# Chunked attention and a feed-forward block: the third tile's first matmul in seven block products throughout

## The chip, the cores and the metric

The kernel runs on one core of a Trainium2 chip. A core has a matrix engine (TensorE, PE in the profile; its weight loads are listed as PEld), a vector engine (VectorE, DVE), an engine for activation functions (ScalarE, ACT), a general one (GpSimd, POOL) and SyncE (SP), which here issues nearly all transfers. Every engine has its own queue and works it off in order; semaphores tie the queues together. SBUF is the core's working memory, PSUM the small memory of eight banks into which TensorE writes.

The metric is the device time of one execution in microseconds. A comparison of two kernels takes runs of both on the same chip.

## The reference

Inputs are q, k, v of shape (8, 8, 576, 64), that is batch, heads, positions, head size, and two matrices w_in (512 x 2048) and w_out (2048 x 512). Attention is inside chunks of 64 positions, and a feed-forward block with the exact GELU follows:

```python
scores = scale * np.matmul(q_c, k_c.transpose(0, 1, 2, 4, 3))   # per chunk of 64 positions
attn = softmax(scores)                                          # over the last axis
x = matmul(attn, v_c)  ->  rows of (batch, position), columns of (head, 64): 4608 x 512
h = x @ w_in                                                    # "mm1", 4608 x 2048
g = 0.5 * h * (1.0 + erf(h * inv_sqrt2))
out = g @ w_out                                                 # "mm2", 4608 x 512, float32
```

## The kernel before

The 4608 rows are worked off as nine tiles of 512 rows: tiles 0 to 7 take the first 512 positions of each batch entry, tile 8 the last 64 positions of all eight. The "third tile" of the change is tile 2. The main loop runs over the tiles `t`; one turn (`phase`) is mm1 of tile `t` with GELU, then mm2 of tile `t`, and between the matmuls of the turn stands the attention of the following tile(s), so that x of tile `t + 1` is ready when the turn ends. The program is written in the order in which each engine is to run it; the framework adds the semaphores.

**Seven products.** From tile 1 on, mm1 is computed by the Winograd form of Strassen's scheme: x, w_in and h are cut into 2 x 2 blocks, and seven block products with sums of blocks stand for eight. `x_sums` makes the sums of x (T1 to T4) on DVE, `w_in_sums` those of w_in once. The columns of h are cut into four groups of two 128-column blocks in each half, called a, b, c and d. A product such as `6a` is four matmuls of 256 columns (L680). For each group: products 1 and 2 build bank X; `c1` copies X (after product 1) to bank Y on ACT, onto which 6, 5 and 3 are added; `c2` (ACT) and `c3` (DVE) take copies of Y on the way; products 7 and 4 build bank Z; `a2` and `a1` (DVE) add Z to those copies; `g..` are the GELUs on ACT that write h. So product 6 needs `c1`, product 5 may only be added once `c2` has read Y, product 3 once `c3` has, and product 4 once `a1` has read Z.

**The order.** Each tile has a string of such words, which `mm1_groups` (L649) follows: `LATE` for tile 1, `THIRD` for tile 2, `FOUR` for tiles 3 to 7, `LAST` for tile 8. In `FOUR` all four groups are in seven products. In the `THIRD` of before, groups a, b and c are, and group d's four 128-column blocks are computed plainly, at the word `p`: four matmuls of 512 columns into one bank (L702) and one GELU (L706). `FOURS` tells for which tiles bank Z lies in the PSUM pool of the transposes and which scratch tiles the groups use.

**What else stands in tile 2's turn.** `extra` ties other work to words of the string; the dictionary `e1` at L1109 to L1123 makes it for tile 2:

- `w_sums((4,))` at the first `1a`: the last of four sums of w_out blocks, one DVE instruction (L743). It is read by mm2 of tile 3, which is in seven products too (mm2 of tile 2 is plain).
- `in_order(3, g)` at the words `i0` to `i3`: k of tile 3 has been transposed by a DMA (`flip`, L197, `k_u<-k_nat`) with its keys in another order than that of the scores; four DVE copies (L205) write them in order to `k_t`. Tile 3 alone needs this here.
- behind the fourth copy (`behind_k`): a copy of one element on POOL (L1116), which holds POOL back until then, the POOL casts of tile 4's q and k to bf16 (L164), the two transposing DMAs of tile 4 on SP (L197), loads of v of tile 4 and q of tile 5, and the casts of v of tile 4 (L217).

In tile 2's mm2 (L867, sixteen slots of four matmuls of 512 columns), the scores of tile 3 (`quad_S`, L246) come ahead of slot 2, their sums on DVE (L270 on) follow, the products with v (L315) come ahead of slot 7, then x of tile 3 and `x_sums(3)`, and the scores of tile 4 in two halves ahead of slots 12 and 13. In tile 3's mm2 the scores of tile 5 follow in the same way.

Of the kernel before, what the change touches and what calls it, by code (L numbers as in the profile page):

```python
# [11 lines left out]
def kernel(  # L12
# [9 lines left out]
    nc = tc.nc  # L22
# [5 lines left out]
    B, H, S, D = q.shape  # L28
    CH = 64
    NC = S // CH  # L30
    J = 4
    PC = CH // J
    G = H // 2
# [56 lines left out]
    tiles = [dict() for _ in range(NT)]  # L90
# [108 lines left out]
    def in_order(t, g):  # L199

        st = tiles[t]
        if "k_u" not in st:
            st["k_u"], st["kt"] = st["kt"], flips.tile([P, G * J, P], bf16, tag="kt", name="k_t")
        raw = st["k_u"]
        DV(st["kt"][:, g * J:(g + 1) * J].rearrange("p n (e j) -> p (n e) j", j=J),  # L205
           raw[:, g * J:(g + 1) * J].rearrange("p j e -> p e j"))

    def cast_v_rows(t, copy, behind=None):
# [256 lines left out]
    def att_sum_pe(t, g):  # L465

        pT = tiles[t]["pT", g]
        sT = ps_at.tile([P, 2, MT // P // 2, 2], f32, tag="at", name="sT")
        for r in range(2):
            for m in range(2):  # L470
                nc.tensor.matmul(sT[:, r, m], pT[:, r, 2 * m:2 * m + 2].rearrange("p n e -> p (n e)"), ones_r[:],
                                 start=True, stop=True)
        rr = work.tile([P, 2, MT // P // 2, 2], f32, tag="rr", name="rr", bufs=2)

        def inverse():
            nc.vector.reciprocal(rr[:], sT[:])

        def spread():
            rc_ps = ps_mm.tile([P, CT // 2, 2, CH], f32, tag="mm", name="rc_ps")
            for m in range(2):  # L480
                for c in range(2):
                    for r in range(2):
                        nc.tensor.matmul(rc_ps[CH * r:CH * (r + 1), 2 * m:2 * m + 2, c],
                                         rr[:, r, m, c:c + 1].to_broadcast([P, D]), ident_f[:],
                                         start=True, stop=True, tile_position=(0, CH * r))
            nc.scalar.copy(rc_of(t, g), rc_ps[:].rearrange("p n c e -> p (n c e)"))
        return inverse, spread
# [27 lines left out]
    DV, AC, PO = nc.vector.tensor_copy, nc.scalar.copy, nc.gpsimd.tensor_copy  # L515
# [40 lines left out]
    FIRST7, FIRST71 = 3, 1  # L556
# [57 lines left out]
    def x_sums(t, which=(1, 3, 2, 4)):  # L614
# [7 lines left out]
        for i in which:  # L622
# [7 lines left out]
    LATE = """begin start sums 1a c1a p 1b 7a c1b 6a 2a c2a 2b g11a 5a 6b g11b c2b c3a a1a 1c c1c 7b 5b g22a 6c 4a  # L630
              c2c 3a c3b a2a 3b 5c 7c g12a a1b c3c 2c 4b 3c a1c g21a g12b 4c g22b a2b a2c g11c g21c g21b g12c
              g22c end"""

    THIRD = """begin 1a c1a p 1b c1b 2a 7a 6a c2a 6b 2b 5a g11a c2b g11b 1c c1c c3a a1a p 5b 4a g22a 6c a2a 2c c3b
               g11c 7b a1b i0 3a c2c 3b 7c g21a 5c i1 c3c a1c g12b g12a g22b p 4b g22c p 4c a2b a2c i2 i3 3c g21b
               g12c g21c"""

    LAST = """begin 1a c1a p 6a 1b c2a c1b 7a 2a 5a 6b g11a c2b c3a 1c 2b c1c g11b 5b a1a g22a 4a 6c 7b c2c 3a a2a
              c3b g21a g12a p a1b 4b 5c g22b 2c a2b 7c g21b g11c 3b c3c 3c a1c 4c g12b a2c h1 g22c g12c g21c p p
              h2 h3"""  # L640
# [1 line left out]
    FOUR = """begin 1a 1b c1a 1c 6a 7a c1b c2a 6b 5a 2a c1c 6c c2b 5b 7b c3a g11a a1a c3b c2c 3a a1b 1d 4a g22a 4b  # L642
               g12a c1d 2b a2a g22b 6d 5c g21a a2b 2d 7c h1 g11b c3c c2d 2c g11d 5d a1c 7d c3d 3c g21b 4c g11c 3b a1d
               g22c 4d g12c g12b 3d a2c a2d g21c g22d g12d g21d h2 h3"""

    FOURS = range(FIRST7, B)
    PROGRAMS = {1: LATE, 2: THIRD, B: LAST, **{t: FOUR for t in FOURS}}

    def mm1_groups(t, extra, between={}):  # L649

# [6 lines left out]
        banks, sums = {}, {}  # L657
        four = t in FOURS
        tags = {"a": ("y_1", "y_2"), "b": ("y_5", "rc" if four else "y_2"), "d": ("y_1", "rc")}
# [28 lines left out]

        for word in PROGRAMS.get(t, PROGRAM).split():
            for u in extra.pop(word, ()):  # L690
# [42 lines left out]
    def w_sums(which):  # L733

        b11, b12 = w_out_sb[:, :FH, :NH], w_out_sb[:, :FH, NH:]
        b21, b22 = w_out_sb[:, FH:, :NH], w_out_sb[:, FH:, NH:]
        for i in (1, 3):
            if i in which:
                pair = wsum.tile([P, 2, FH, NH], bf16, tag="wsum", name="w_t")
                w_t[i], w_t[i + 1] = pair[:, 0], pair[:, 1]  # L740
        of = {1: (b12, b11), 3: (b22, b12), 2: (b22, w_t[1]), 4: (b21, w_t.get(2))}
        for i in which:
            nc.vector.tensor_tensor(w_t[i], *of[i], op=mybir.AluOpType.subtract)  # L743
# [178 lines left out]
    def pool_cast_k(t):  # L922
        pool_cast_q(t, "k")
# [42 lines left out]
    with tc.manual_schedule():  # L966
# [33 lines left out]
        i2, p2 = att_sum_pe(0, 2)  # L1000
# [4 lines left out]
        i3, p3 = att_sum_pe(0, 3)  # L1005
# [62 lines left out]
        def flips_of(n):  # L1068
            for nm in "qk":
                flip(n, nm)  # L1070
# [22 lines left out]
        for t in range(1, NT):  # L1093
            e1, e2 = {}, {}
            n = t + 1
            if n < NT:
                tiles[n]["x"] = xpool.tile([P, G, MT], bf16, tag="x", name="x")
            if t == 1:
                flips_of(2)
                load_v_rows(2, (1,))  # L1100
                def behind_sums():
                    w_in_sums(slice(0, 2), "c")
                    cast_v_rows(2, PO, w_s["c", 4][:, 0, 0, 0:1])
                    loads_of_qk(3)
                    pool_cast_qk(3)
                e1 = {"1a": [behind_sums], "p": [lambda: load_v_rows(3)], "end": [lambda: w_sums((1, 3, 2))]}
                e2 = one_tile(2, {5: [lambda: act_table(Act.Gelu)],
                                  8: [lambda: flips_of(3), lambda: loads_of_qk(4)]})
            elif t == 2:  # L1109
                cast_v_rows(3, PO)  # L1110
                e1 = {f"i{g}": [lambda g=g: in_order(3, g)] for g in range(G)}
                e1["1a"] = [lambda: w_sums((4,))]

                def behind_k():
                    in_order(3, G - 1)
                    nc.gpsimd.tensor_copy(tiles[4]["q"][:, 0, 0, 0, 0:1], tiles[3]["kt"][:, G * J - 1, 0:1])  # L1116
                    pool_cast_qk(4)
                    flips_of(4)
                    load_v_halves(4)
                    load_qk(5, "q")  # L1120
                    cast_v_rows(4, PO)
                e1[f"i{G - 1}"] = [behind_k]
                e2 = one_tile(3, {8: [lambda: load_qk(5, "k")], 12: [lambda: quad_S(4, (0,))], 13: [lambda: quad_S(4, (1,)), lambda: act_table(Act.Gelu)]})  # L1123
            elif n < NT:
                def ahead(t=t):
                    if t + 2 < NT:
                        flips_of(t + 2)
                    if t < B - 2:
                        load_v_halves(t + 2, (0,))
                    if t in (FIRST7 + 1, FIRST7 + 2):  # L1130
                        cast_v_rows(t + 1, PO)
                    if t == B - 1:
                        load_v_halves(B, (1,))
                        cast_v_rows(B, PO)

                def next_q(t=t):
                    if t + 3 < NT:
                        load_ahead(t, "q")
                        if t + 3 < B:
                            pool_cast_q(t + 3)  # L1140

                def next_k(t=t):
                    load_ahead(t, "k")

                def rest_of_v(t=t):
                    if t < B - 2:
                        load_v_halves(t + 2, (1,))
                    if t == B - 2:
                        load_v_halves(B, (0,))
                    if t + 3 == B:  # L1150
                        cast_v_rows(t + 2, PO)
                e1 = {"begin": [ahead]}
                if t + 2 < NT:
                    e1["begin"] = [lambda t=t: pool_cast_k(t + 2), ahead]
                if t + 2 == B:
                    def behind_sums(t=t):
                        nc.gpsimd.tensor_copy(tiles[B]["q"][:, 0, 0, 0, 0:1], tiles[t]["s", 2][:, 0, 0:1])
                        pool_cast_q(B)
                        pool_cast_k(B)
                        ahead()  # L1160
                    e1 = {"g11b": [behind_sums]}
                if t == FIRST7:
                    pool_cast_q(t + 2)
                e2 = {1: [lambda: rows_av(n, tiles[n - 1]["Z"]), lambda: rows_x(n)], 2: [], 3: [], 4: [lambda: x_sums(n)]}
                e2[2] += [next_q, next_k, rest_of_v] if t + 3 < B else [rest_of_v, next_q]
                if t + 3 == B:
                    e2[4] += [next_k]
                if n + 1 < NT:
                    e2[1] = [lambda: act_table(Act.Exp)] + e2[1]
                    e2.setdefault(2 if t == FIRST7 else (2, 0), []).extend([lambda: quad_S(n + 1), lambda: act_table(Act.Gelu)])  # L1170
            phase(t, e1, e2, between=last_rows if t == 1 else {})
# [28 lines left out]
```

## Time and profile before

| | us |
|---|---|
| median of three runs | 271.54 (271.02 to 272.47) |
| the profiled execution, its own time | 271.71 |
| its span, first to last instruction | 269.6 |
| PE busy | 260.6 (97%) |
| DVE busy | 201.8 (75%) |
| ACT busy | 186.8 (69%) |
| POOL busy | 78.8 (29%) |

In the lines by time, the first number is the start in microseconds from the span's start, the second how long the group of like instructions took from its first start to its last end, then engine, line, operation, output<-inputs, shape and count; in square brackets how long the engine was idle before, and what ended that. Matmuls overlap, so the time from one group's start to the next is what they cost. SPq is SP's queue of DMA issues: the number there is the time of the issuing, not that of the transfer. In the table by stage (the line that begins with core 0 names its columns), each line is a stretch of time with its length, the busy microseconds of each engine with the count of instructions, the granted clock of TensorE as a share of full speed, the mean share of the DMA engines, and GB/s.

### The profile page before, as it was taken

The page shows a single profiled execution, that of the slowest core. Times are in us where ns is not written, and L with a number is a line of the kernel's source. Part 1 is how long each engine was busy: PE and PEld are TensorE (multiplying, and loading weights), DVE is VectorE, ACT ScalarE, POOL GpSimd, SP SyncE. Part 2 cuts the span into 40 slices and gives each one's busy share as a digit, 9 for nine tenths or more (in the row PEclk, how much of TensorE's full clock was granted, in tenths as well). Part 3 has the DMA queues.
Part 4 walks back from the last instruction along what each step waited for, and adds up shares of the span by engine and source line. Part 5 has one row for each costly group of instructions (what it writes and reads, how often), then busy time and mean ns, then how long its engine had stood idle before and what let it go on. Part 6 is the DMA issues. An engine that isn't in the chain of part 4 may idle for free.

```text
span 269.6 us, 7526 instructions
## 1 busy us (share of the span) xinstructions
PE 260.6 (97%) x3080; PEld 193.8 (72%) x3080; DVE 201.8 (75%) x368; ACT 186.8 (69%) x363; POOL 78.8 (29%) x127
## 2 busy tenths in 40 slices
PE   7989999999999999999999999999999999999993
PEld 2554454486458554888888888888888888888782
DVE  2663787969898779699669966996799669956852
ACT  3567756788767867897589669957895799238600
POOL 2734668350271061215026003711053030000000
PEclk9999999999999999999999999999999999999999
DMA  6999999899989999996999999997797760430005
GB/s 217 254 362 405 395 396 242 225 270 189 320 207 162 269 233 233 300 191 138 200 271 257 232 204 239 270 185 175 221 212 165 191 166 0 91 139 7 0 4 157
DMA packets 127075, 56.59 MB, mean 210 GB/s; under 512 B 103488, under 2 KB 120896, under 8 KB 127040
## 3 DMA queue, kind: packets, MB, share of 16 engines
q1 hardware_dynamic: 126592, 55.59, 81.7%
q10 hardware_dynamic: 448, 0.52, 0.7%
q8 instruction: 24, 0.39, 0.7%
q14 instruction: 11, 0.09, 0.1%
HBM read 36.70 MB, written 9.44 MB: 171 GB/s over the span
## 4 chain that ended last, share of the span: by engine, by line
PE 67%; SPq 11%; DMA 10%; POOL 4%; DVE 2%; issue 2%; ACT 1%; POOLq 0%; ACTq 0%; DVEq 0%
PE y_ps L749 24%; PE h_Y L680 11%; PE h_Z L680 8%; PE h_X L680 7%; PE y_ps L867 6%; SPq L120 5%; DMA arrival<-in_moe_w_out_dram 5%; PE h_ps L537 4%; PE y_ps L758 4%; DMA arrival<-in_moe_w_in_dram 2%; SPq L149 2%; DMA k_u<-k_nat 2%; SPq L108 2%; PE s_ps L246 2%; POOL w_out_sb L948 1%
## 5 line engine op out<-in xcount | busy, mean ns | idle before, releaser
L680 PEld LDWEIGHTS <-w_in_s 128*128 128x128 bf16 x464 | 45.2, 98 | 6.6 <-DVE x_t L624 0.5
L680 PEld LDWEIGHTS <-w_in_sb 128*128 128x128 bf16 x348 | 33.9, 98 | 7.8 <-issue 1.6
L867 PE MATMUL y_ps<-w_out_sb,h 128*128 128x512 bf16 x144 | 33.0, 380 | 0.0
L680 PE MATMUL h_X<-x,w_in_sb 128*128 128x256 bf16 x232 | 32.6, 272 | 0.0
L164 POOL CAST q_nat<-arrival 128x512 bf16<-128x512 f32 x33 | 19.7, 638 | 43.1 <-DMA arrival<-in_q_dram 42.9
L749 PEld LDWEIGHTS <-h_s 128*128 128x128 bf16 x304 | 29.8, 98 | 3.4
L680 PE MATMUL h_Y<-x_t,w_in_s 128*128 128x256 bf16 x232 | 31.8, 272 | 0.2 <-DVE x_t L624 0.2
L749 PEld LDWEIGHTS <-h 128*128 128x128 bf16 x288 | 27.9, 98 | 3.5
L164 POOL CAST k_nat<-arrival 128x512 bf16<-128x512 f32 x34 | 23.1, 716 | 20.9 <-DMA arrival<-in_k_dram 16.8
L217 POOL CAST v_nat<-arrival 128x1024 bf16<-128x1024 f32 x14 | 15.1, 1088 | 46.7 <-DMA arrival<-in_v_dram 46.6
L749 PE MATMUL y_ps<-w_t,h_s 128*128 128x256 bf16 x208 | 24.8, 273 | 0.0
L867 PEld LDWEIGHTS <-h 128*128 128x128 bf16 x144 | 13.3, 98 | 15.0 <-issue 0.2
L749 PE MATMUL y_ps<-w_out_sb,h 128*128 128x256 bf16 x192 | 22.9, 273 | 0.0
L964 ACT ACT_TABLE_LOAD x16 | 20.5, 1283 | 1.0 <-PEq L1184 0.7
L717 ACT COPY h_Y<-h_X 128x512 f32<-128x512 f32 x29 | 16.5, 583 | 2.8 <-PE h_X L680 2.6
L687 ACT ACTIVATE h<-h_Y 128x512 bf16<-128x512 f32 x29 | 17.1, 593 | 1.9 <-PE h_Y L680 1.3
L687 ACT ACTIVATE h<-h_X 128x512 bf16<-128x512 f32 x29 | 17.2, 597 | 1.4 <-PE h_X L680 0.8
L680 PE MATMUL h_Z<-x_t,w_in_sb 128*128 128x256 bf16 x116 | 16.9, 272 | 0.7 <-DVE h_sb L731 0.5
L680 PE MATMUL h_Z<-x_t,w_in_s 128*128 128x256 bf16 x116 | 17.4, 273 | 0.0
L680 PE MATMUL h_Y<-x,w_in_s 128*128 128x256 bf16 x116 | 16.9, 272 | 0.0
L728 DVE COPY h_a<-h_Y 128x512 f32<-128x512 f32 x8 | 5.5, 692 | 14.6 <-PE h_Y L680 14.6
L253 ACT ACTIVATE pT<-s_ps 128x512 bf16<-128x512 f32 x28 | 14.5, 601 | 2.3 <-PE s_ps L246 2.3
(145 smaller groups left out, 494.2 us busy)
## 6 DMA issues: line engine op xcount, KB each, us to landing
arrival<-in_q_dram SPq DMA_DIRECT2D x7, 1024.0 KB
arrival<-in_k_dram SPq DMA_DIRECT2D x24, 256.0 KB
out_dram<-y_sb SPq DMA_DIRECT2D x23, 256.0 KB
arrival<-in_v_dram SPq DMA_DIRECT2D x20, 256.0 KB
arrival<-in_moe_w_out_dram SPq DMA_DIRECT2D x4, 1024.0 KB
arrival<-in_v_dram SPq DMA_DIRECT2D x30, 128.0 KB
out_dram<-y_sb SPq DMA_DIRECT2D x5, 512.0 KB
arrival<-in_moe_w_in_dram SPq DMA_DIRECT2D x4, 512.0 KB
```

The source lines that it names most:

```text
L120: nc.sync.dma_start(to, rows.rearrange("h key d -> key h d"))
L164: copy(st[nm][:, g].rearrange("p j r d -> p r j d"), st[nm + "f"][:, 2 * g:2 * g + 2])
L217: copy(st["v"][:, part[0], part[1], :D], st["vf"][:, part[0], part[1]])
L253: nc.scalar.activation(pT[:].rearrange("p u (c j) -> p u c j", j=J), s_ps[g2][c][:].rearrange("p u (j c) -> p u c j", j=J), Act.Exp, scale ...
L537: nc.tensor.matmul(h_ps[a][:], w_in_sb[:, ks, f * P:(f + 1) * P], st["x"][:, ks, :], start=(ks == 0), stop=(ks == KS - 1))
L680: nc.tensor.matmul(banks[g + name][:, i], lhs[:, kk, i], rhs[:, kk], start=fresh and i == kk == 0, stop=(kk == 1), skip_group_check=True)
L687: nc.scalar.activation(h[:, j:j + 2, m], src[:], Act.Gelu)
L717: AC(banks[g + "Y"][:], banks[g + "X"][:])
L749: nc.tensor.matmul(out[m], lhs[:, f, m * P:(m + 1) * P], rhs[:, f, :], start=fresh and f == 0 and (m == 0 or len(out) == 3), stop=(f == FH ...
L758: nc.tensor.matmul(out[m], lhs[:, f, m * P:(m + 1) * P], rhs[:, f, :], start=False, stop=(f == FH - 1), skip_group_check=True)
L867: nc.tensor.matmul(y_ps[:], st["h"][:, f, ms * P:(ms + 1) * P], w_out_sb[:, f, :], start=(f == 0), stop=(f == FF - 1))
L964: nc.scalar.activation(act_scratch[:], rest[:, 0:1], func)
```

## The change

`THIRD` is now `FOUR` with its beginning in another order (products 1a 1b 1c 2a ahead of 7a 6a, since the sums of x come late in tile 2), and tile 2 counts among `FOURS`. The four plain blocks are gone; group d is computed in seven products like the others. The four copies that put k of tile 3 in order run on POOL, all at the beginning of mm1, in POOL's queue behind the casts of v of tile 3 and ahead of the casts of q and k of tile 4; the copy of one element is gone. `w_sums((4,))` stands at the word `h2`, the end of mm1, behind the last sum of group d. The order of SP's DMA issues is the same.

```diff
-        DV(st["kt"][:, g * J:(g + 1) * J].rearrange("p n (e j) -> p (n e) j", j=J),
+        PO(st["kt"][:, g * J:(g + 1) * J].rearrange("p n (e j) -> p (n e) j", j=J),
            raw[:, g * J:(g + 1) * J].rearrange("p j e -> p e j"))
...
-    THIRD = """begin 1a c1a p 1b c1b 2a 7a 6a c2a 6b 2b 5a g11a c2b g11b 1c c1c c3a a1a p 5b 4a g22a 6c a2a 2c c3b
-               g11c 7b a1b i0 3a c2c 3b 7c g21a 5c i1 c3c a1c g12b g12a g22b p 4b g22c p 4c a2b a2c i2 i3 3c g21b
-               g12c g21c"""
...
-    FOURS = range(FIRST7, B)
-    PROGRAMS = {1: LATE, 2: THIRD, B: LAST, **{t: FOUR for t in FOURS}}
+    THIRD = FOUR.replace("6a 7a c1b c2a 6b 5a 2a", "c1b 2a 7a 6a c2a 6b 5a")
+
+    FOURS = range(FIRST7 - 1, B)
+    PROGRAMS = {1: LATE, 2: THIRD, B: LAST, **{t: FOUR for t in range(FIRST7, B)}}
...
-                e1 = {f"i{g}": [lambda g=g: in_order(3, g)] for g in range(G)}
-                e1["1a"] = [lambda: w_sums((4,))]
 
                 def behind_k():
-                    in_order(3, G - 1)
-                    nc.gpsimd.tensor_copy(tiles[4]["q"][:, 0, 0, 0, 0:1], tiles[3]["kt"][:, G * J - 1, 0:1])
+                    for g in range(G):
+                        in_order(3, g)
                     pool_cast_qk(4)
...
-                e1[f"i{G - 1}"] = [behind_k]
+                e1 = {"begin": [behind_k], "h2": [lambda: w_sums((4,))]}
```

## The prediction

> **What bounds the kernel now.** I read the page first, then a table of busy time by stage, the PE's waits, the instructions in order of time around tile 2's first matmul stage (mm1), and last the transfers that the PE meets behind it.
>
> ```profile
> span 269.6 us, 7526 instructions
> PE 260.6 (97%) x3080; PEld 193.8 (72%) x3080; DVE 201.8 (75%) x368; ACT 186.8 (69%) x363; POOL 78.8 (29%) x127
> ```
>
> The PE is the bound: it is busy for 97% of the span and no other engine passes 75%. Only what shortens the PE's own work, or a place where it waits, can move the end. The stages, cut where the PE goes from one to the next (mm1 of tile 2, mm2 of tile 2, mm1 of tile 3):
>
> ```profile
> core 0: us, PE busy (x) PEld busy (x) DVE busy (x) ACT busy (x) POOL busy (x), PEclk, DMA share, GB/s
> 78.94:92.34 13.40, 12.87 (x102) 9.78 (x101) 10.78 (x18) 9.87 (x19) 2.02 (x2) 1.00 1.08 215
> 92.34:108.66 16.32, 16.32 (x258) 7.85 (x256) 13.43 (x27) 12.77 (x31) 6.01 (x11) 1.00 0.99 226
> 108.66:121.03 12.37, 12.37 (x113) 10.94 (x112) 9.11 (x16) 11.09 (x22) 3.35 (x5) 1.00 0.88 255
> ```
>
> Tile 2's mm1 takes 13.40 us, of which the PE is idle 0.53. Tile 3's mm1 already has the form that tile 2 is to get, and takes 12.37 with no idle PE. The clock is full in all three and the DMA engines are taken nearly all the time. Where the 0.53 comes from:
>
> ```profile
> PE h_Z L680 <- DVE h_sb L731: 0.5, 1, 0.5
> 88.96 1.13 DVE L205 COPY k_t<-k_u 128x512 bf16<-128x512 bf16 x2 [1.12 <-DMA k_u<-k_nat]
> 90.00 0.69 DVE L728 COPY h_sb<-h_Y 128x512 f32<-128x512 f32 x1
> 90.72 0.69 DVE L731 TENSOR_TENSOR h_sb<-h_Z,h_sb 128x512 f32<-128x512 f32 x1
> 91.47 0.60 PE L680 MATMUL h_Z<-x_t,w_in_sb 128*128 128x256 bf16 x4 [0.53 <-DVE h_sb L731]
> ```
>
> DVE stands at the first two copies that put k of tile 3 in order until the transposed k lands. The copy and sum of group c are queued behind them, and product 4c on the PE waits for that sum.
>
> **The change, part by part.**
>
> *Seven products everywhere (THIRD from FOUR, L634).* Durations on the PE:
>
> ```profile
> 79.38 1.03 PE L702 MATMUL h_ps<-x,w_in_sb 128*128 128x512 bf16 x4
> 80.24 1.04 PE L680 MATMUL h_X<-x,w_in_sb 128*128 128x256 bf16 x8
> 81.11 0.60 PE L680 MATMUL h_Z<-x_t,w_in_s 128*128 128x256 bf16 x4
> 81.55 1.04 PE L680 MATMUL h_Y<-x_t,w_in_s 128*128 128x256 bf16 x8
> 82.24 0.59 ACT L728 COPY h_a<-h_Y 128x512 f32<-128x512 f32 x1 [0.71 <-PE h_Y L680]
> ```
>
> From start to start a plain block costs 0.86 (79.38 to 80.24), a product 0.437 (80.24 to 81.55 holds three). Four plain blocks (3.44) give way to seven products (3.06): 0.38 less. The whole stage is then 28 x 0.437 = 12.24; tile 3 needs 0.13 more for it.
>
> The order at the stage's beginning isn't tile 3's, though: products 1a 1b 1c 2a stand ahead of 7a 6a, and 6b 5a behind. 5a adds to the bank that the copy c2a on ACT has to have read, and c2a follows 6a. Starting at 78.94, 6a is sixth and starts at 81.13; c2a starts 0.69 behind it (81.55 to 82.24 above), at 81.82, and ends at 82.41. 5a, the eighth, would be due at 82.00: a new wait of 0.4 to 0.45. In the old order 2b stood between them and hid it. 5a then also comes one product later than in tile 3, and a chain on DVE hangs on it:
>
> ```profile
> 110.84 1.05 PE L680 MATMUL h_Y<-x_t,w_in_s 128*128 128x256 bf16 x8
> 112.00 0.69 DVE L728 COPY h_a<-h_Y 128x512 f32<-128x512 f32 x1 [2.45 <-PE h_Y L680]
> 114.12 0.69 DVE L731 TENSOR_TENSOR h_b<-h_Z,h_b 128x512 f32<-128x512 f32 x1
> 114.86 0.60 PE L680 MATMUL h_Z<-x_t,w_in_sb 128*128 128x256 bf16 x4
> ```
>
> In tile 3, 5a (second half of the first row) starts at 111.28, c3a a1a c3b a1b follow on DVE, and 4b starts at 114.86, 0.05 behind a1b: 3.58 after 5a. In tile 2, 5a at 82.45 puts 4b at 86.03 at the earliest. 4b is fifteenth, due at 78.94 + 14 x 0.437 + 0.45 = 85.51, or 85.61 with 0.1 for 6c behind c1c: a second wait, 0.3 to 0.4. Behind it the order is tile 3's, which has no wait. ACT gets two instructions more (eight gelus, a copy of each kind for group d, against four plain gelus less: 24 for 22); tile 3 carries 24 beside a 12.37 us stage. Sum: 12.24 + 0.45 + 0.1 + 0.35 = 13.14, and 13.27 with all of tile 3's 0.13; some of that falls into the new waits, so I take 13.2. The stage ends at 92.14 instead of 92.34: 0.2 gained, though 0.38 of work and 0.53 of waiting leave it.
>
> *k in order on GpSimd, no DVE copies (L205), no one-element copy (L1116).* The 0.53 goes with it. On POOL:
>
> ```profile
> 93.94 0.19 POOL L1116 COPY q_nat<-k_t 128x1 bf16<-128x1 bf16 x1 [11.87 <-DVE k_t L205]
> 94.20 2.29 POOL L164 CAST q_nat<-arrival 128x512 bf16<-128x512 f32 x4
> 97.84 2.29 POOL L164 CAST k_nat<-arrival 128x512 bf16<-128x512 f32 x4 [1.35 <-DMA arrival<-in_k_dram]
> 121.44 3.63 POOL L164 CAST k_nat<-arrival 128x512 bf16<-128x512 f32 x4 [5.50 <-DMA arrival<-in_k_dram]
> 92.71 1.11 DVE L205 COPY k_t<-k_u 128x512 bf16<-128x512 bf16 x2
> 94.16 0.74 PE L246 MATMUL s_ps<-q_t,k_t 64*64 64x64 bf16 x64
> ```
>
> No row shows this gather on POOL. Its nearest rows are casts of as many elements: four take 2.29 alone (0.57 each) and 3.63 beside a busy DVE (0.91). On DVE the copy took 0.56. I take 0.6 and keep 0.56 to 0.91 as ends. Four behind k's landing at 88.96 end at 91.4 (92.6 at the dear end). The reader is the score product of tile 3, which starts 1.82 behind mm1's end, at 93.96: covered by 1.3 to 2.5. Queued behind the copies are the q casts of tile 4, which now start at 91.4 to 92.6 instead of 94.20, and the k casts, which wait for their arrival at 97.84 in either case. So POOL's k cast doesn't move.
>
> *The last w_out sum (L743) at word h2.*
>
> ```profile
> 81.68 1.46 DVE L743 TENSOR_TENSOR w_t<-w_out_sb,w_t 128x2048 bf16<-128x2048 bf16 x1
> 96.12 0.45 DVE L270 STREAM_TRANSPOSE pt<-pT 128x256 f32<-128x256 f32 x1 [2.30 <-ACT pT L253]
> ```
>
> It takes the place of the two DVE copies of 1.11 at mm1's end: 0.35 more, inside the 2.30 that DVE idles ahead of 96.12. Without that cover it would cost 0.35. It now lies beside POOL's q casts, and the 3.63 above is what such neighbours do to four casts: 1.34 more. The Trainium skill says the same of its kind in GPSIMD Engine Reference, section 1: POOL's SBUF interface is shared with VectorE, and VectorE instructions with two SBUF inputs contend. By that rule this sum, with two SBUF inputs, slows the casts; the rows agree. The casts then end between 95.0 and 96.2, ahead of the 96.49 of before.
>
> **What meets the PE next.** A fifth of a microsecond survives only if the transfers behind it aren't late:
>
> ```profile
> 94.26 1.24 SPq L883 DMA_DIRECT2D out_dram<-y_sb  x2
> 96.52 2.74 SPq L197 DMA_TRANSPOSE q_t<-q_nat  x1
> 100.16 1.59 SPq L197 DMA_TRANSPOSE k_t<-k_nat  x1
> 104.33 0.34 PEld L246 LDWEIGHTS <-k_t 64*64 64x64 bf16 x32 [0.42 <-DMA k_t<-k_nat]
> 125.10 1.70 SPq L197 DMA_TRANSPOSE k_t<-k_nat  x1
> 128.98 0.63 PEld L246 LDWEIGHTS <-k_t 64*64 64x64 bf16 x64 [0.21 <-DMA k_t<-k_nat]
> 121.41 0.68 DVE L575 TENSOR_TENSOR h_s<-h 128x1024 bf16<-128x1024 bf16 x1
> ...
> 123.89 0.71 DVE L576 TENSOR_TENSOR h_s<-h_s,h 128x512 bf16<-128x512 bf16 x1
> 134.76 0.76 DVE L624 TENSOR_TENSOR x_t<-x 128x512 bf16<-128x512 bf16 x2
> 134.91 1.47 PE L680 MATMUL h_X<-x,w_in_sb 128*128 128x256 bf16 x12
> ```
>
> At 104.33 and 128.98 the weight loader's last event was the landing of k of tiles 4 and 5, at most 0.42 and 0.21 ahead of it. By the second pair a flip takes at most 3.88, so the first had landed by 104.04; the PE, 0.2 earlier, comes at 104.13 and doesn't wait. k of tile 5 landed between 128.77 and 128.98, and the PE now comes at 128.78: between 0 and 0.2 goes back. That landing hangs on POOL's cast at 121.44 (121.44 + 3.63 = 125.07, then the flip), which waits for its load and not for the PE. DVE's sums beside this cast (the first and last of four stand here, 121.41 to 124.60) come 0.2 earlier, which may end it about 0.1 earlier (1.34 lost over 3.2). I take 0.05 as given back and 0.15 as the gain. The sums of x for tile 4's mm1 stand right behind DVE's earlier work at 134.76, and move with the PE's. Behind tile 3 nothing changes.
>
> The profiled execution took 271.71; 271.71 - 0.15 = 271.56. The median of the runs, 271.54, is 0.17 lower, so as a median I write 271.4.
>
> **Rivals.**
> - *Tile 2 becomes tile 3.* No new waits, and transfers that move along: 13.40 - 12.37 = 1.03, 270.5. For it: the same program in the same kernel. Against it: the two waits above, and k of tile 5, which caps the gain at 0.21 unless it lands earlier. Even whole this is 0.38%, under the 0.5% (1.36 us) that a measurement of this kernel can tell from no change.
> - *Slower: the gather is dear on POOL.* Place: the score product at 93.96, less 88.96, leaves 5.0 for four copies, 1.25 each; above that every 0.1 costs the PE 0.4. From 1.6 each the kernel is slower by over 0.5%, at 2.0 each it is 274.3. Against it: the copies of equal size at 0.57 to 0.91. The Trainium skill advises VectorE for elementwise work (GPSIMD Engine Reference, section 3.1) with 2.6 cycles an element at 1.2 GHz for its dearest plain loop: an estimate from the page of 1.1 each, by which the PE still doesn't wait.
> - *Slower: k of tile 4 or 5 lands later.* The q flip leaves when SP is free of the stores at 94.26, at 95.5 instead of 96.52, among loads of k for tile 4 that still arrive, and the PE's own code is fetched at other moments. With at most 0.42 and 0.21 of slack, a delay of 1 us in either landing costs 0.6 to 1.0: 272.2. It decides above 0.5%, with 1.5 us or more of delay: 273.
> - *The change does nothing that lasts:* the 0.2 is given back whole at 128.98: 271.5. Its time is that of the forecast.
>
> **Chances.** Forecast with the fourth case 0.62, tile 2 as tile 3 0.14, dear gather 0.08, later landing 0.16. The forecast's own range is 270.9 to 272.0. Faster by over 0.5% takes 1.36 us, more than the whole mechanism holds; only some of the second case with a scatter like that of the three runs (271.02 to 272.47) gets there: 0.09. Slower takes most of the dear gather, half of the late landing and some scatter: 0.19. Same 0.72. The range goes from 270.2 (the second case with scatter) to 273.1 (a landing 1.5 us late).
>
> **What would show it.** Right: mm1 of tile 2 about 13.2 long, no wait on h_sb, a wait of 0.4 ahead of 5a and 0.3 ahead of 4b, four POOL copies of about 0.6 from 88.9, DVE's 1.46 sum ahead of the first transpose of tile 3, and the weight loader still released by k at about 128.9. Wrong: a POOL copy above 1.2, a PE wait at the score products, an mm1 of 12.4, or a stage behind tile 3 that changes its length.

## The result and the profile after

The changed kernel takes 273.75 us (median; 272.24 to 275.32) against 271.55 for the kernel before (270.73 to 272.75): a ratio of 1.008, 95% interval 1.0054 to 1.0105. It is slower; the forecast was 271.4 with a range up to 273.1. The ratios in this document leave out the few runs in which the chip was in a slower state, and they are not simply the quotient of the two medians. The profiled execution takes 273.3, with a span of 271.2 against 269.6.

The first line of the page of the kernel after:

```profile
span 271.2 us, 7560 instructions
```

The table by stage of the kernel after: mm1 and mm2 of tile 2, mm1 of tile 3, then mm1 of tiles 4, 5 and 6 (columns as in the table of before).

```profile
core 0: us, PE busy (x) PEld busy (x) DVE busy (x) ACT busy (x) POOL busy (x), PEclk, DMA share, GB/s
78.95:93.02 14.07, 12.98 (x114) 10.91 (x112) 11.54 (x18) 10.79 (x21) 7.31 (x9) 1.00 1.11 248
93.02:109.50 16.48, 16.39 (x258) 7.94 (x256) 13.62 (x26) 12.95 (x31) 8.17 (x12) 1.00 1.02 245
109.50:121.87 12.37, 12.37 (x113) 10.94 (x112) 9.40 (x16) 11.09 (x22) 4.89 (x9) 1.00 0.99 243
135.75:148.69 12.94, 12.58 (x114) 10.93 (x112) 10.16 (x18) 11.53 (x22) 6.96 (x11) 1.00 1.09 236
162.57:175.24 12.67, 12.49 (x114) 10.93 (x112) 9.89 (x18) 11.57 (x22) 7.13 (x12) 1.00 1.05 250
189.12:202.25 13.13, 12.54 (x114) 10.85 (x112) 10.65 (x19) 11.41 (x22) 4.15 (x7) 1.00 0.74 212
```

The same table of the kernel before, for the three later stages:

```profile
134.91:147.30 12.39, 12.39 (x115) 10.94 (x113) 9.60 (x18) 11.41 (x22) 5.83 (x11) 1.00 1.09 283
161.18:173.88 12.70, 12.49 (x115) 10.94 (x113) 9.92 (x18) 11.57 (x22) 7.19 (x12) 1.00 1.03 258
187.76:200.54 12.78, 12.55 (x115) 10.84 (x113) 10.30 (x18) 11.42 (x22) 3.72 (x6) 1.00 0.77 214
```

The clock is full everywhere. Against before, mm1 of tile 2 is 0.67 longer (14.07 for 13.40), its mm2 0.16, mm1 of tile 4 0.55, of tile 6 0.35, of tile 5 0.03 shorter: 1.70 in all, for a span that is 1.6 longer. In this profile 0.67 of it sits in the stage that was changed and 0.16 in the mm2 behind it, a little under half together; the rest sits in stages whose program the change leaves as it was. The PE's waits in this stretch of the kernel after:

```profile
PE h_Y L678 <- DVE x_t L624: 1.2, 2, 0.6
PE h_Z L678 <- DVE h_d L729: 0.5, 2, 0.4
PE h_Y L678 <- ACT h_a L726: 0.3, 1, 0.3
PE h_Z L678 <- DVE h_b L729: 0.2, 1, 0.2
```

The last two are the waits that the prediction expected ahead of 5a and of 4b. The first two were not expected: the sums of x are waited for once in tile 2 and once behind tile 3, 0.6 each, and h_d twice behind tile 3. The instructions in order of time at the beginning of tile 2's mm1, kernel after, for the PE, DVE and POOL:

```profile
81.95 1.03 PE L678 MATMUL h_Y<-x_t,w_in_s 128*128 128x256 bf16 x8 [0.58 <-DVE x_t L624]
83.28 1.60 PE L678 MATMUL h_Y<-x_t,w_in_s 128*128 128x256 bf16 x12 [0.29 <-ACT h_a L726]
86.85 0.60 PE L678 MATMUL h_Z<-x_t,w_in_sb 128*128 128x256 bf16 x4 [0.22 <-DVE h_b L729]
...
79.54 1.19 DVE L624 TENSOR_TENSOR x_t<-x 128x512 bf16<-128x512 bf16 x2
80.65 1.71 DVE L624 TENSOR_TENSOR x_t<-x,x_t 128x512 bf16<-128x512 bf16 x2
82.28 0.68 DVE L876 COPY y_sb<-y_ps 128x512 f32<-128x512 f32 x1
...
77.97 2.48 POOL L164 CAST k_nat<-arrival 128x512 bf16<-128x512 f32 x4 [0.42 <-DMA arrival<-in_k_dram]
80.40 1.23 POOL L217 CAST v_nat<-arrival 128x1024 bf16<-128x1024 f32 x1
82.30 1.05 POOL L217 CAST v_nat<-arrival 128x1024 bf16<-128x1024 f32 x1 [0.67 <-DMA arrival<-in_v_dram]
```

DVE's four sums of x (7a reads the second, 6a the third, 4a the last) take 1.19 and 1.71 a pair, 2.9 in all, while POOL does the last cast of k and the first of v of tile 3. Undisturbed, a pair takes 0.75 to 0.88 (the runs e6 to e10 below). 6a therefore starts 0.58 late, and since the plain blocks are gone and 2b stands far behind, the PE has nothing else ready. DVE's next instruction, a copy out of PSUM, takes its usual 0.68 although the second cast starts 0.02 behind it.

In tile 4 the same thing happens at another place. Kernel after, in order of time:

```profile
143.53 2.37 POOL L217 CAST v_nat<-arrival 128x1024 bf16<-128x1024 f32 x2
143.30 0.50 DVE L575 TENSOR_TENSOR h_s<-h 128x512 bf16<-128x512 bf16 x1
143.84 1.15 DVE L576 TENSOR_TENSOR h_s<-h_s,h 128x512 bf16<-128x512 bf16 x1
147.82 0.60 PE L678 MATMUL h_Z<-x_t,w_in_sb 128*128 128x256 bf16 x4 [0.36 <-DVE h_d L729]
```

And the kernel before, at the same instructions:

```profile
146.05 2.06 POOL L217 CAST v_nat<-arrival 128x1024 bf16<-128x1024 f32 x2
142.46 0.41 DVE L575 TENSOR_TENSOR h_s<-h 128x512 bf16<-128x512 bf16 x1
142.90 0.42 DVE L576 TENSOR_TENSOR h_s<-h_s,h 128x512 bf16<-128x512 bf16 x1
```

The casts of v of tile 5 start 7.78 behind mm1's start after, and 11.14 before. DVE's first two sums of h start 7.55 and 8.0 to 8.1 behind it in both: in the one execution they meet the casts, in the other not. In tile 6 it is the sums of x and the cast of v of tile 7, in the kernel after:

```profile
189.18 1.60 DVE L624 TENSOR_TENSOR x_t<-x 128x512 bf16<-128x512 bf16 x2
189.24 1.27 POOL L217 CAST v_nat<-arrival 128x1024 bf16<-128x1024 f32 x1 [7.52 <-DMA arrival<-in_v_dram]
```

But the same collision is in the kernel before:

```profile
188.13 1.73 DVE L624 TENSOR_TENSOR x_t<-x,x_t 128x512 bf16<-128x512 bf16 x2
187.89 1.23 POOL L217 CAST v_nat<-arrival 128x1024 bf16<-128x1024 f32 x1 [5.54 <-DMA arrival<-in_v_dram]
```

What differs in tile 6 is that the first sum of x starts 0.06 behind mm1's start after, and 0.30 ahead of it before. So the wait ahead of 6a is 0.58 instead of 0.23, which is the 0.35 of this stage. What makes these sums later is not shown.

### The profile page after: what moved, and what is told of

Read it like the earlier page. It is cut to its first block, busy times and chain, and to the rows that moved or that the text cites. A ratio compares the mean times of both kernels' runs of the same rounds, so it can differ in the third digit from the quotient of the medians.

```text
span 271.2 us, 7560 instructions
## 1 busy us (share of the span) xinstructions
PE 261.3 (96%) x3092; PEld 195.3 (72%) x3092; DVE 201.2 (74%) x367; ACT 188.0 (69%) x365; POOL 81.8 (30%) x130
## 4 chain that ended last, share of the span: by engine, by line
PE 62%; DVE 16%; SPq 6%; DMA 5%; ACT 5%; issue 3%; POOL 1%; DVEq 0%; ACTq 0%; POOLq 0%
PE y_ps L747 20%; PE h_Y L678 12%; PE h_Z L678 8%; PE h_X L678 7%; PE h_ps L537 4%; PE y_ps L890 4%; PE y_ps L756 3%; DMA arrival<-in_v_dram 2%; DMA arrival<-in_moe_w_in_dram 2%; SPq L149 2%; ACT h L685 2%; DVE x_t L624 2%; DVE part L273 2%; DVE x L322 2%; DVE rc L308 2%
## 5 line engine op out<-in xcount | busy, mean ns | idle before, releaser
L678 PEld LDWEIGHTS <-w_in_s 128*128 128x128 bf16 x480 | 46.8, 98 | 8.3 <-issue 1.2
L678 PEld LDWEIGHTS <-w_in_sb 128*128 128x128 bf16 x360 | 35.1, 98 | 7.5 <-issue 1.7
L164 POOL CAST q_nat<-arrival 128x512 bf16<-128x512 f32 x33 | 20.5, 659 | 47.6 <-DMA arrival<-in_q_dram 47.5
L678 PE MATMUL h_Y<-x_t,w_in_s 128*128 128x256 bf16 x240 | 32.6, 272 | 1.5 <-DVE x_t L624 1.2
L678 PE MATMUL h_X<-x,w_in_sb 128*128 128x256 bf16 x240 | 33.5, 273 | 0.0
L164 POOL CAST k_nat<-arrival 128x512 bf16<-128x512 f32 x34 | 21.3, 664 | 17.8 <-DMA arrival<-in_k_dram 11.8
L865 PEld LDWEIGHTS <-h 128*128 128x128 bf16 x144 | 13.3, 98 | 15.0 <-issue 0.2
L685 ACT ACTIVATE h<-h_Y 128x512 bf16<-128x512 f32 x30 | 17.7, 592 | 1.9 <-PE h_Y L678 1.5
L678 PE MATMUL h_Z<-x_t,w_in_sb 128*128 128x256 bf16 x120 | 17.5, 272 | 0.8 <-DVE h_d L729 0.5
L678 PE MATMUL h_Z<-x_t,w_in_s 128*128 128x256 bf16 x120 | 18.0, 272 | 0.0
L678 PE MATMUL h_Y<-x,w_in_s 128*128 128x256 bf16 x120 | 17.7, 273 | 0.0
```

Of the source, the lines that this page charges most:

```text
L164: copy(st[nm][:, g].rearrange("p j r d -> p r j d"), st[nm + "f"][:, 2 * g:2 * g + 2])
L678: nc.tensor.matmul(banks[g + name][:, i], lhs[:, kk, i], rhs[:, kk], start=fresh and i == kk == 0, stop=(kk == 1), skip_group_check=True)
L685: nc.scalar.activation(h[:, j:j + 2, m], src[:], Act.Gelu)
L865: nc.tensor.matmul(y_ps[:], st["h"][:, f, ms * P:(ms + 1) * P], w_out_sb[:, f, :], start=(f == 0), stop=(f == FF - 1))
```

## The experiments

The theory from these rows: (a) the change's order has nothing ready at the beginning of mm1 when a sum of x is lengthened, and so lets through a collision that the old order covered better; (b) the later stages lose by the same kind of collision, whose place is set by when loads arrive. The rivals: the gather on POOL costs the time, or the w_out sum at h2, or the later stages differ by chance alone. Every kernel below computes everything. A run's time in the text is a median, and the ratio is to the kernel before on the same chip. The runs come in four groups, each on one chip: after; before_again, e2, e3 and e6; after_again and e7 to e9; e10 to e13. A summary, with the lengths out of tables by stage like those above; "x sums" is when the last sum of x ends behind mm1's start in tile 2:

| run | ratio (95% interval) | mm1 of tile 2 | x sums | mm1 of tiles 4, 5, 6 |
|---|---|---|---|---|
| before, profile of the first run | 1 | 13.40 | 2.22 | 12.39 12.70 12.78 |
| before_again | 1.0004 (0.9972 to 1.0037) | 12.70 | 2.85 | 13.60 12.80 12.81 |
| e2_pool_only | 0.9984 (0.9953 to 1.0015) | 12.86 | 2.97 | 12.47 12.43 12.65 |
| after | 1.0080 (1.0054 to 1.0105) | 14.07 | 3.41 | 12.94 12.67 13.13 |
| after_again | 1.0032 (0.9996 to 1.0068) | 13.62 | 2.86 | 13.65 13.16 13.13 |
| e3_w_early | 1.0044 (1.0014 to 1.0073) | 13.53 | 2.85 | 13.34 13.05 13.13 |
| e6_v_behind_x | 1.0034 (1.0008 to 1.0061) | 13.25 | 2.11 | 13.44 13.22 12.39 |
| e7_after_hold | 0.9983 (0.9953 to 1.0012) | 13.26 | 2.12 | 12.77 12.82 12.39 |
| e8_before_hold | 0.9985 (0.9954 to 1.0017) | 13.48 | 2.11 | 12.39 12.47 12.39 |
| e9_pool_hold | 0.9999 (0.9972 to 1.0026) | 12.70 | 2.13 | 12.39 12.57 12.39 |
| e10_pool_hold456 | 0.9991 (0.9957 to 1.0024) | 12.70 | 2.14 | 12.39 12.43 12.39 |
| e11_after_hold456 | 1.0017 (0.9994 to 1.0041) | 13.86 | 3.10 | 12.38 12.81 12.39 |
| e12_mended_hold456 | 0.9998 (0.9971 to 1.0025) | 12.57 | 2.22 | 12.42 12.39 12.39 |
| e13_before_hold456 | 0.9983 (0.9960 to 1.0007) | 12.71 | 2.98 | 12.39 12.45 12.39 |

**The kernel before once more** (no edit).

> The kernel before once more, for a second profile of it. Theory A (the loss comes from tile 2's mm1: the new order has nothing between the sums of x on DVE and the products that read them, and POOL's casts of v stretch those sums): mm1 of tile 2 takes 13.3 to 13.5 us here whether or not the casts fall on the sums, because its plain block stands ahead of 6a. Theory B (the loss comes from later stages, which the changed timing of POOL and of the transfers disturbs): the stages of tiles 4 and 6 keep their 12.38 and 12.78 us here too. If those stages vary by 0.4 or more from one execution of the same kernel to the next, what after shows there is not the change's.

It takes 272.36 against 271.73, a ratio of 1.0004. Its profile, though, isn't that of the first run. The table by stage, mm1 of tile 2 and of tile 4:

```profile
79.53:92.23 12.70, 12.60 (x99) 9.77 (x100) 11.15 (x18) 10.27 (x20) 1.67 (x2) 1.00 0.99 252
134.81:148.41 13.60, 12.81 (x115) 10.91 (x113) 10.83 (x18) 11.54 (x22) 6.84 (x11) 1.00 1.09 265
```

and in order of time, the casts of v of tile 5:

```profile
142.17 2.25 POOL L217 CAST v_nat<-arrival 128x1024 bf16<-128x1024 f32 x2
```

Two things follow. The wait of 0.53 on k in tile 2, from which the forecast got its gain, is not in this execution: the profile names no wait of the PE in the stage, which takes 12.70 for 13.40. And the casts start 7.36 behind mm1's start in tile 4, and that stage takes 13.60 for 12.39, in the kernel before too. Both theories miss here: A had 13.3 to 13.5 for the first stage, B had 12.38 for the second. One profile can't tell which stages "change their length".

**The k copies on GpSimd alone.** The order of before stays, and the w_out sum stays at 1a:

```diff
-        DV(st["kt"][:, g * J:(g + 1) * J]...
+        PO(st["kt"][:, g * J:(g + 1) * J]...
...
-    THIRD = """... 7b a1b i0 3a ... 5c i1 c3c ... a2b a2c i2 i3 3c ...
+    THIRD = """... 7b a1b 3a ... 5c c3c ... a2b a2c 3c ...
...
-                    in_order(3, G - 1)
-                    nc.gpsimd.tensor_copy(tiles[4]["q"][:, 0, 0, 0, 0:1], tiles[3]["kt"][:, G * J - 1, 0:1])
+                    for g in range(G):
+                        in_order(3, g)
...
-                e1[f"i{G - 1}"] = [behind_k]
+                e1["begin"] = [behind_k]
```

> Only the move of the four k copies to POOL (and the one-element copy gone); order of products and place of the w_out sum as before. Theory A: the wait on h_sb is gone and the old order still covers the sums of x, so mm1 of tile 2 falls from 13.40 to 12.4 to 12.9 us and the kernel is 0.3 to 0.9 us faster than before (ratio 0.997 to 0.999). Theory B: slower than before by 0.8 to 2 us, with the loss in tiles 3 to 6.

271.31, ratio 0.9984: the gather doesn't cost the time, and a gain isn't shown either, since the interval holds 1. In order of time, at tile 2's beginning, DVE and POOL, with the stage's row out of the table:

```profile
79.42 1.59 DVE L624 TENSOR_TENSOR x_t<-x 128x512 bf16<-128x512 bf16 x2
79.36 1.05 POOL L217 CAST v_nat<-arrival 128x1024 bf16<-128x1024 f32 x1
```

```profile
78.83:91.69 12.86, 12.76 (x100) 9.67 (x101) 10.41 (x16) 10.28 (x20) 5.40 (x7) 1.00 1.02 225
```

Here too the cast lies on a sum of x, the first as in after_again, and the sums end 2.97 behind mm1's start, later than the 2.86 there. The old order needs 12.86 with it, 0.16 more than the 12.70 of the runs where the sums are undisturbed (e9, e10). The change's order needs 13.62, 0.37 more than its undisturbed 13.25 (e6 below). The collision is not new; the old order covered more of it. That is one execution: in before_again and e13 (12.70 and 12.71) only the last sum is lengthened, which 4a alone reads, much later.

**The w_out sum at 1a again**, in the changed kernel:

```diff
-                e1 = {"begin": [behind_k], "h2": [lambda: w_sums((4,))]}
+                e1 = {"begin": [behind_k], "1a": [lambda: w_sums((4,))]}
```

> After, with the last w_out sum back at the first 1a, the only difference to after. Theory A: the sum of 1.46 us stands on DVE ahead of c3a and can only add to tile 2's mm1: 14.1 to 14.6 us there, 2 to 2.7 us slower than before in all. Theory B: the same as after or up to 1 us better, if the sum at mm1's end, beside POOL's q casts, is what shifts the later work.

273.4, ratio 1.0044: the loss stays, and mm2 of tile 2 stays at 16.48 as in the changed kernel. The sum at h2 isn't the cause of either. mm1 of tile 2 takes 13.53, not the 14.1 to 14.6 of theory A.

**The casts of v of tile 3 held behind the sums of x of tile 2**, in the changed kernel (a copy of one element out of the last sum, ahead of the casts in POOL's queue):

```diff
-                cast_v_rows(3, PO)
+                cast_v_rows(3, PO, tiles[2]["T"][4][:, 0, 0:1])
```

> After, with POOL's casts of v of tile 3 held by a one-element copy until the sums of x of tile 2 are made. Theory A: the sums take 0.84 and 0.87 us again, the wait of 0.58 ahead of 6a is gone, mm1 of tile 2 takes 13.1 to 13.5 us instead of 14.07, and the kernel is 0.6 to 0.9 us faster than after (1.3 to 1.6 us over before). Theory B: mm1 of tile 2 may shorten, but the total stays within 0.4 us of after.

272.96, ratio 1.0034. The stage and the DVE's sums in it:

```profile
79.00:92.25 13.25, 12.74 (x114) 10.93 (x113) 10.24 (x18) 10.78 (x21) 5.74 (x8) 1.00 1.06 223
```

```profile
79.53 0.78 DVE L624 TENSOR_TENSOR x_t<-x 128x512 bf16<-128x512 bf16 x2
80.23 0.87 DVE L624 TENSOR_TENSOR x_t<-x,x_t 128x512 bf16<-128x512 bf16 x2
```

Without the collision the sums end at 2.11 and the change's order takes 13.25, the 13.2 of the prediction. Over the executions of this order the stage follows the end of the sums: 2.11, 2.85, 2.86, 3.10, 3.41 go with 13.25, 13.53, 13.62, 13.86, 14.07 (in the second of these, e3, only the last sum is long and the w_out sum also stands on DVE; its excess is a wait of 0.40 for 0.22 ahead of 4b). That is part (a). For the whole time nothing is shown: the changed kernel was not run in this group, and e3, which was, is only 0.4 slower with an overlapping interval. In the profile, mm1 of tiles 4 and 5 is long again (13.44, 13.22) and mm2 of tile 2 grows to 16.87, with a wait of 0.49 on k of tile 4.

**The changed kernel once more, and three kernels with four holds.** The holds: v of tile 3 as above, v of tiles 5 and 6 behind the first sums of h of tiles 4 and 5, v of tile 7 behind the sums of x of tile 6.

```diff
-                    if t in (FIRST7 + 1, FIRST7 + 2):
-                        cast_v_rows(t + 1, PO)
...
-                    if t + 3 == B:
-                        cast_v_rows(t + 2, PO)
...
+                if t in (FIRST7 + 1, FIRST7 + 2):
+                    e1["g11b"] = [lambda t=t: cast_v_rows(t + 1, PO, tiles[t]["s", 2][:, 0, 0:1])]
...
+                    e2[5] = [lambda t=t: cast_v_rows(t + 2, PO, tiles[t + 1]["T"][4][:, 0, 0:1])]
```

> The changed kernel once more, on the chip of the next three and with a second profile. Theory A+C (the new order costs 0.3 to 0.9 us in tile 2's mm1; and the later start of the following stages moves DVE's two-input sums under POOL's casts of v, which stretches those sums from 0.42 to 1.15 us and makes the PE wait in tiles 4 to 6): mm1 of tile 2 at 13.2 to 14.1, and each of the mm1 of tiles 4, 5 and 6 above 12.4 whenever a cast of v lies on a sum; 1.2 to 2.2 us slower than before.

> After, with POOL's casts of v of tiles 3, 5, 6 and 7 each held by a one-element copy until DVE's sums of that stage (x of tile 2, first h sums of tiles 4 and 5, x of tile 6) are made. Theory C (collisions of these casts with DVE's sums cost tiles 4 to 6): mm1 of tiles 4, 5, 6 take 12.4 to 12.5 us each, and 1 to 1.6 us of after's time goes. If the later losses have another cause (a transfer, a PSUM bank), they stay and the time stays within 0.7 us of after.

> Before, with the same four holds. Theory C: tiles 4, 5, 6 at 12.4 to 12.5 us here too; 0.5 to 1 us faster than before and a smaller spread from run to run. The difference of e7 to this one is then tile 2's mm1 alone: 0.1 to 0.6 us. If the collisions come from the change alone, holding gains nothing here.

> Only the k copies on POOL (as in e2), with the same four holds: the old order of products without its wait on k. Theory A+C: mm1 of tile 2 at 12.4 to 12.9, tiles 4 to 6 at 12.4 to 12.5; 0.8 to 1.4 us faster than before, the fastest of all. If the wait on k was worth nothing, it equals e8.

On this chip the kernel before takes 271.77. The changed kernel takes 273.11 (1.0032, interval 0.9996 to 1.0068): the loss is less clear than in the first runs. With the four holds it takes 271.76 (0.9983): 1.35 less. Its three later stages sum to 37.98 with the holds and to 39.94 without, its mm1 of tile 2 takes 13.26 for 13.62. Two of the three stages stay above the 12.4 to 12.5 that was expected: in tiles 4 and 5 (12.77, 12.82) POOL's casts of k, which are not held, lie on the first sums of h (in tile 4 they run from 141.38 to 143.86, and the sums at 142.62 and 143.42 take 0.76 and 0.71). On the kernel before, the same holds show no gain (271.65, 0.9985), nor with the k copies on GpSimd (271.89, 0.9999), where 0.5 to 1.4 had been expected, though they bring mm1 of tiles 4 to 6 to 12.39 to 12.57. The PE's waits of these two kernels, the first of the kernel before with the holds and the second of the one with the copies on GpSimd, say where it went:

```profile
PE s_ps L246 <- DVE x L322: 1.3, 1, 1.3
```

```profile
PE s_ps L246 <- DMA k_t<-k_nat: 1.1, 1, 1.1
```

In the second, k of tile 4 lands late. In the first DVE's x is named, but the weight loader of the same kernel waited for k as well:

```profile
PEld L246 <- DMA k_t<-k_nat: 1.8, 1, 1.8
```

mm2 of tile 2 grows to 17.67 and 17.49 from 16.32. These two kernels differ from e13 and e10, where it is 16.32, in the hold in tile 2's turn alone; the hold keeps POOL back, and behind POOL stand the loads and flips of the next tiles. In e7, with the same hold in the change's order, mm2 takes only 16.54; why k isn't late there isn't known.

**Three holds (tiles 4 to 6 alone), on four kernels.** The last of the four has THIRD in a mended order as well: 2a ahead of 7a and 6a, 2b ahead of 5a, 5c ahead of 4b, so that a product stands ready behind each of the three places that wait:

```diff
-    THIRD = FOUR.replace("6a 7a c1b c2a 6b 5a 2a", "c1b 2a 7a 6a c2a 6b 5a")
+    THIRD = " ".join(FOUR.split())
+    for a, b in (("6a 7a c1b c2a 6b 5a 2a", "c1b 2a 7a 6a c2a 6b 2b 5a"), ("c1d 2b a2a", "c1d a2a"),
+                 ("4a g22a 4b g12a c1d a2a g22b 6d 5c", "4a g22a 5c g12a c1d 4b a2a g22b 6d")):
...
+        THIRD = THIRD.replace(a, b)
```

> The kernel before with the k copies on GpSimd and the sum of w_out where it was, and the v casts of tiles 5, 6 and 7 (not of tile 3) held behind the first sums of h or of x. If the lengthened VectorE sums under the v casts are what the later stages lose, mm1 of tiles 4, 5 and 6 reads 12.4 each (37.2 in sum, 37.54 in the run of the k copies alone), mm1 of tile 2 stays at 12.7 to 12.9, mm2 of tile 2 at 16.3 (its cast is not held, so k of tile 4 is not late as in the run with four holds), and the time is about 270.9 us (270.3 to 271.5), ratio 0.997. Rival, the holds only move the collision to the k loads: mm2 of tile 4 or 5 grows over 13.9, or PE waits on k_t, and the time is 271.5 or more.

> The changed kernel with the three later holds and tile 3's v casts left where the change has them. If two separate losses add up (tile 2's x sums, and the h sums of tiles 4 to 6), this gives back the later one alone: mm1 of tile 2 stays at 13.6 to 14.1, mm1 of tiles 4, 5 and 6 sum to 37.2 to 38.0 instead of 38.7 to 39.9, and the time is 272.0 us (271.5 to 272.5), ratio 1.001, between the changed kernel (1.003 to 1.008) and the one with all four holds (0.998). Rival, all of it is the later stages: the same time as with four holds. Rival, all of it is tile 2: the changed kernel's time.

> The kernel before with the three later holds alone. Before already had mm1 of tile 4 at 12.39 in one execution and 13.59 in another; if the holds take the chance out of it, mm1 of tiles 4, 5 and 6 reads 12.4 each, mm1 of tile 2 12.7 to 13.4 by when k lands, mm2 of tile 2 16.3, and the time is 271.2 us (270.6 to 271.8), ratio 0.998. Rival, what the holds gain comes back as late loads: PE waits on k_t and the ratio is 1 or more.

> As the run before it in this list (changed kernel, three later holds), with seven products in another order in tile 2: plain blocks of other work stand ahead of the blocks that need the sums of x and of h (2a ahead of 6a and 7a, 2b ahead of 5a, 5c ahead of 4b). If the loss in tile 2 is that the change's order has nothing ready while a lengthened x sum runs, mm1 of tile 2 reads 12.5 without a collision and 13.3 with one, 0.7 less than the order of the change in the same condition, and the time is about 271.3 us (270.8 to 271.9). Rival, the loss in tile 2 is not the order: mm1 of tile 2 stays at 13.6 to 14.1 and the time equals that of the run with three holds.

On one chip, where the kernel before takes 271.88: before with three holds 271.30, with the k copies on GpSimd too 271.17, the change with three holds 272.16, and with the mended order 271.61. The table by stage of the change with three holds, and of the mended order (mm1 and mm2 of tile 2):

```profile
78.35:92.21 13.86, 12.90 (x113) 10.92 (x112) 11.23 (x18) 10.78 (x21) 6.93 (x8) 1.00 1.10 245
92.21:108.69 16.48, 16.40 (x259) 7.95 (x257) 13.95 (x25) 12.94 (x31) 8.16 (x12) 1.00 1.06 245
```

```profile
79.52:92.09 12.57, 12.57 (x113) 10.93 (x112) 10.25 (x18) 10.49 (x21) 5.32 (x6) 1.00 1.12 249
92.09:108.57 16.48, 16.43 (x259) 7.95 (x256) 13.71 (x26) 12.95 (x31) 8.12 (x12) 1.00 1.03 241
```

In the tables by stage the two losses are separate: with the later stages held (12.38, 12.81 and 12.39), tile 2's is left (13.86, waits of 0.4, 0.3 and 0.2 on x, h_a and h_b). The times alone don't tell this run from the one with four holds, since the intervals overlap. In the mended order the profile names no wait of the PE in this stage, and it takes 12.57. But its sums of x were undisturbed in this execution (2.22), so what is shown is 12.57 for 13.25 in the same condition; the 13.3 expected with a collision was not met. Against the old order with k copies on GpSimd, seven products at their best save 0.13 in mm1 (12.57 for 12.70) and lose 0.16 in mm2 (16.48 for 16.32): nothing is left. All four intervals overlap, and the holds on the kernel before (0.9983, 0.9960 to 1.0007) aren't shown to beat it.

## Why the prediction was wrong

*The stage's length with the change.* The step "I take 13.2" comes out where the sums of x are undisturbed: 13.25 and 13.26. The two new waits it rests on are there, but shorter: 0.29 ahead of 5a for 0.4 to 0.45, and 0.22 ahead of 4b for 0.3 to 0.4. So the agreement is partly luck, as two errors cancel: 0.51 of waits stood for 0.8, and 12.74 of PE time (in e6) for 12.34 to 12.47. The gain of 0.38 in PE work was too large as well: without a named wait the old order takes 12.70 (e9, e10) and seven products 12.57 (e12), 0.13 less.

*What failed first: the sums of x as a constant.* The working placed 6a "sixth" with its operands in time. The change puts 7a and 6a behind four products without a plain block ahead, where POOL's casts (of v, in after and e11 also the last of k) make one sum or two last 0.6 to 1.25 instead of 0.42. With the measured ends of the sums the stage is 13.5 to 14.07, so 0.3 to 0.8 of the loss is this term, and it was taken as zero. The prediction saw the neighbour in one direction only: DVE slows POOL's casts (the 3.63). The Trainium skill says in GPSIMD Engine Reference, section 1, that the SBUF interface is shared with VectorE and that VectorE instructions with two SBUF inputs contend; the traces agree: such a sum goes from 0.42 to 1.25, and a copy out of PSUM keeps its 0.68. The prediction applied it to the w_out sum and the q casts beside it (1.30 and 3.29 measured), and not to the sums that the PE waits for.

*What failed second: the 0.53 wait on k as a fixed part of before.* It is 0.53 and 0.6 in two executions of the old order with the DVE copies (before, e8), and missing in two others (before_again and e13, where no wait of the PE is named in this stage and it takes 12.70 and 12.71). The copies start 10.0 and 10.1 behind mm1's start in the first two, 8.8 and 8.9 in the others, so the removal of the wait is worth 0 to 0.6, by when k lands. The change's undisturbed 13.25 therefore is a gain of 0.15 against one execution and a loss of 0.55 against others: against those, the plain blocks were worth more as cover than the PE work that they cost.

*What failed third: "Behind tile 3 nothing changes".* mm1 of tiles 4 and 6 grew by 0.55 and 0.35. In tile 4 a POOL cast now lies on DVE's sums of h; in tile 6 it lies on the sums of x in both kernels, and the sums start later. In tile 4 the size goes with the moment of the cast. Behind mm1's start it comes at 7.1 to 7.8 in five executions (before_again among them), which take 12.94 to 13.65; at 8.48 in e2, 12.47; at 11.14 in before, 12.39. What sets the moment is POOL's chain of q, k and v casts, whose first step waits for a load:

```profile
137.11 2.30 POOL L164 CAST q_nat<-arrival 128x512 bf16<-128x512 f32 x4 [15.96 <-DMA arrival<-in_q_dram]
```

That is 1.36 behind mm1's start in the kernel after, and 4.65 in before by the same row there. Whether the change makes the load arrive earlier, or these executions happened to differ, isn't settled: without a hold in tile 4 the early cast stands in four of four profiles with the change's order and in one of three with the old one, which is too few. But the record points to the first profile of before as the exception. The holds in tiles 4 to 6 stand behind this first step, so e10 and e13 show it in the old order too: there the q casts start 1.27 and 1.72 behind mm1's start, in before_again 1.31, in e2 2.25. SP issues the load of this q 1.63 ahead of mm1's start in before, and 4.4 to 5.5 ahead in these four, in after, after_again, e3 and e6; of the other profiles only e9, where k of tile 4 lands late, has it as close to mm1's start (2.25). That holding the casts takes most of the loss out of these stages is shown (e7 to e13, from 12.4 to 12.8 a stage).

*The gather on POOL.* In the kernel after, in order of time, with DVE's w_out sum:

```profile
89.44 4.17 POOL L205 COPY k_t<-k_u 128x512 bf16<-128x512 bf16 x4 [6.09 <-DMA k_u<-k_nat]
93.55 3.29 POOL L164 CAST q_nat<-arrival 128x512 bf16<-128x512 f32 x4
93.39 1.30 DVE L741 TENSOR_TENSOR w_t<-w_out_sb,w_t 128x2048 bf16<-128x2048 bf16 x1
```

A copy takes 1.04, outside the 0.56 to 0.91 that was given and near the 1.1 that the prediction estimated from the Trainium skill (GPSIMD Engine Reference, section 3.1). There the 2.6 cycles are for an instruction with two inputs, and this copy has one, so the nearness proves little. The point from which it decides was 1.25, and the PE does not wait at tile 3's scores; the size was off and the conclusion held. The w_out sum lies in DVE's idle time as forecast.

*The transfers.* The slack on k of tiles 4 and 5 didn't come to bear in the kernel after. A wait on k of tile 4 came only with the hold in tile 2. The rival "k of tile 4 or 5 lands later" gave the right sign for a reason that didn't occur.

*What the prediction put at nothing: a later end of ACT's work.* mm2 of tile 2 takes 16.48 instead of 16.32 in the profiles with seven products and an unheld cast in that tile. Set beside before instruction by instruction, the whole 0.16 is one step, at the second half of tile 4's score products. In the kernel after:

```profile
105.78 0.69 DVE L322 TENSOR_TENSOR x<-av_ps,rc 128x512 bf16<-128x512 f32 x1
106.52 0.45 PE L246 MATMUL s_ps<-q_t,k_t 64*64 64x64 bf16 x32
```

These products start 0.05 behind the end of DVE's product for x, in after_again, e3, e11 and e12 as well; in e7 the profile names this instruction as what they wait for:

```profile
PE s_ps L246 <- DVE x L322: 0.2, 1, 0.2
```

The products are due 13.34 behind mm2's start. DVE's instruction ends 13.45 behind it in after and 13.29 in before. The 0.16 runs back along DVE's chain to ACT: the last GELU of mm1 ends 1.91 behind mm2's start in after and 1.75 in before, and the exponentials and DVE's sums follow at the same distances. The prediction counted ACT's two more instructions (24 for 22) and gave them no cost. All this is read from the traces: no run takes the wait away, and that it is these two instructions that make ACT end later is likely but not shown.

## What to carry to other kernels

Before a stage's plain, independent work is taken out, look at what it covers: list the waits that would appear if each operand came as late as its producer's slowest row in any stage, not as in the quiet one. When an engine's elementwise work is read as a price, look at what the neighbouring engine does at that moment, in both directions. And take a second profile of the unchanged kernel before a stage's idle time is counted as a gain; here one stage was 12.39 and 13.60 in two executions of the same program.

## What was not expected of the hardware

A DVE sum of two bf16 operands in SBUF (128x512) takes 0.42. When a POOL cast of 1024 elements lies on it, it takes up to 1.29, and in most of these collisions 1.13 to 1.28. What decides is which of the two starts first. Between 60 and 205 us of the fourteen profiles, 41 such sums start while a cast of v runs; 39 of them end 0.27 or 0.28 behind the cast, whether they started 0.03 or 0.82 behind its start. The other way round, 42 of these casts start under such a sum, and 36 of them end 0.90 to 0.92 behind it; they take up to 1.35 instead of 1.05. Beside a longer sum a cast loses more: the four q casts that start 0.16 behind the w_out sum in the kernel after take 3.29 instead of 2.29. DVE's copies and sums with an operand in PSUM keep their 0.68 and 0.69 beside such casts. On POOL a strided bf16 copy of 512 elements takes 1.04, where a cast of as many elements from f32 takes 0.57.
